# A gated recurrence with top-k experts: contiguous tiles for the transposes, logits in four column groups, exponentials in two batches

## The chip, the cores and the metric

The kernel runs on one core of a Trainium2 chip. The metric is the device time of one execution in microseconds; lower is better. The times given are the median of several runs. One execution was also recorded by the hardware profiler, and the rows below come from that one.

## The reference

Four sequences of 5056 tokens with 256 channels go through a gated recurrence; its output is the input of a mixture of 8 experts, of which each takes only the 80 tokens with the largest gates.

```python
sig = 1.0 / (1.0 + np.exp(-f_logit))
f = lower_bound + (1.0 - lower_bound) * sig
for t in range(S):
    h = f[:, t] * h + (1.0 - f[:, t]) * x[:, t]
    y[:, t] = h
x = y.reshape(B * S, D)                      # 20224 x 256
logits = x @ w_gate                          # 20224 x 8
expert_idx = np.argmax(logits, axis=1)
gate_w = softmax(logits)[arange, expert_idx]
for e in range(8):                           # keep the 80 largest gates of each expert
    h = np.maximum(x[tok_idx] @ w1[e], 0.0)
    out[tok_idx] = gate_w[tok_idx, None] * (h @ w2[e])   # all other rows are zero
```

All of it is in fp32.

## The kernel before

The program has three stages. The first is the recurrence stage. It works on units: 512 tokens of one of the four sequences, with all 256 channels. Four units, one for each sequence, make a group; there are 10 groups and 40 units. The last group of a sequence ends with the sequence and overlaps the one before.

A unit goes through these steps, each a small function that issues its instructions. `load` brings f_logit and x into SBUF through the SP queue; a partition gets four consecutive tokens, 4 KB in one piece. `gate` is a sigmoid on ScalarE (s_t). `enter` multiplies it with x on GpSimd (u_t). `to_channels` transposes both on TensorE, eight 128x128 transposes each, into PSUM tiles sp and up; as a partition holds four consecutive tokens, each transpose writes every fourth column. `decay` makes the factor a from sp on ScalarE, two instructions. `scan` runs the recurrence along 512 tokens on VectorE, two instructions of 128 channels each (shown as one row with x2), into h. `to_tokens` transposes h back with eight transposes into PSUM tiles hp, in two halves of four; ScalarE copies the first half to ht, VectorE the second, and the SP queue stores ht to DRAM. `logits` multiplies h with the gate weights: the weights that the array holds are 128 tokens of h (every fourth column), and 8 columns of wg are streamed. An fp32 product is two passes on TensorE, so the 8 products of a unit are 16 matmuls in the trace.

Once per group, `gates` takes the logits of 4 x 512 tokens: the maximum (mx), the difference from it (sh), an exponential on ScalarE (ex), the first column that reaches the maximum (eq, rv, oh), the sum and its reciprocal (sm, gt), and the gate in the column of its expert (gm). `candidates` transposes gm on TensorE (ct) and copies it to its columns of cand on VectorE.

The order of the instructions on each engine is that in which the program issues them: one loop runs over the units, and each round issues the load of the unit four ahead, the gate and enter of the unit two ahead, to_channels and decay of the next unit, the scan of this unit, to_tokens and logits of the unit before, and the group's steps one and two units later. PSUM has eight banks; before the change sp and up have two buffers each, hp two, and lg and ct one each.

The second stage finds the 80 largest of each row of cand, in ten rounds on VectorE, then again over the lists of one expert; meanwhile the SP queue loads the expert weights and writes zeros to the output. The third stage gathers the chosen tokens, runs the experts on TensorE and scatters the results. Lines 278 to 375 are not changed except for comments.

Of the kernel before, what the change touches and what calls it, by code (L numbers as in the profile page):

```python
# [16 lines left out]
P = 128  # L17
# [5 lines left out]
def kernel(  # L23
# [27 lines left out]
    # The last group of a sequence ends with it and overlaps the one before,  # L51
    # of which only the rows in front of the overlap are used.
# [6 lines left out]
    def rows(g):  # L59
        return used(g) // R  # L60

# [13 lines left out]
    wg = consts.tile([P, DC, E], F32, name="wg")  # L75
    nc.scalar.dma_start(out=wg, in_=w_gate.rearrange("(o p) e -> p o e", p=P))
# [6 lines left out]
    # Candidate row e * C + b * R + r holds the tokens b * S + 4 * pos + r.  # L83
# [8 lines left out]
    cand = consts.tile([P, SEG], F32, name="cand")  # L92
    ctx.enter_context(tc.manual_schedule())

    with tc.tile_pool(name="ld", bufs=5) as ld, \
         tc.tile_pool(name="sup", bufs=3) as sup, \
         tc.tile_pool(name="apool", bufs=2) as apool, \
         tc.tile_pool(name="hpool", bufs=B + 3) as hpool, \
# [6 lines left out]
        xs, fs, sts, uts, sps, ups, decays, hs, lgs, gms = ({} for _ in range(10))  # L105
# [10 lines left out]
        def load(n):  # L116
            g, b = divmod(n, B)
            fs[n] = ld.tile([P, R, D], F32, name="f_t", tag="f_t")
            nc.sync.dma_start(
                out=fs[n], in_=f_logit[b, ds(first(g), G)].rearrange("(p r) d -> p r d", r=R))  # L120
# [12 lines left out]
        def to_channels(n, src, dst, tag):  # L133
            for o in range(DC):
                ps = psu.tile([P, P, R], F32, name=tag, tag=tag)
                for r in range(R):
                    nc.tensor.transpose(ps[:, :, r], src[n][:, r, ds(o * P, P)], ident)  # L137
                dst[n, o] = ps.rearrange("c p r -> c (p r)")
            del src[n]

        # h / (1 - lower_bound) is what runs through the scan.
# [15 lines left out]
        def to_tokens(n):  # L157
            g, b = divmod(n, B)
            n_p = rows(g)
            ht = htok.tile([P, R, D], F32, name="ht", tag="ht")  # L160
            hv = hs[n].rearrange("c o (p r) -> c o p r", r=R)
            half = R // 2
            for i in range(2):
                hp = ptp.tile([P, half, D], F32, name="hp", tag="hp")
                for r in range(half):
                    for o in range(DC):
                        nc.tensor.transpose(hp[:n_p, r, ds(o * P, P)],  # L167
                                            hv[:, o, :n_p, i * half + r], ident)
                copy = nc.scalar.copy if i == 0 else nc.vector.tensor_copy
                copy(ht[:n_p, ds(i * half, half)], hp[:n_p])  # L170
            nc.sync.dma_start(
                out=h_dram[ds(b * S + first(g), n_p * R)].rearrange("(p r) d -> p r d", r=R),
                in_=ht[:n_p])

        def logits(n):
            g, b = divmod(n, B)
            n_p = rows(g)
            if b == 0:
                lgs[g] = plg.tile([P, C, E], F32, name="lg", tag="lg")
            hv = hs[n].rearrange("c o (p r) -> c o p r", r=R)  # L180
# [6 lines left out]
        def gates(g):  # L187
            n_p = rows(g)
            lg = lgs.pop(g)[:n_p]
# [7 lines left out]
            sh = small([C, E], "sh")  # L197
            nc.vector.tensor_tensor(sh, lg, mx.unsqueeze(2).broadcast_to(full), ALU.subtract)  # L198
            ex = small([C, E], "ex")
            nc.scalar.activation(ex, sh, ACT.Exp)  # L200
# [6 lines left out]
            oh = small([C, E], "oh")  # L207
            nc.vector.tensor_tensor(oh, eq, rv.unsqueeze(2).broadcast_to(full), ALU.is_equal)
            sm = small([C], "sm")
            nc.vector.tensor_reduce(sm, ex, AX.X, ALU.add)  # L210
# [3 lines left out]
            gm = small([E, C], "gm")  # L214
            nc.vector.tensor_tensor(gm.rearrange("p e c -> p c e"), oh,
# [191 lines left out]
```

## Time and profile before

| | us |
|---|---|
| median of 3 runs | 553.43 (553.03 to 557.71) |
| span of the profiled execution, first to last instruction | 552.3 |
| TensorE busy in the span | 399.0 |
| VectorE busy | 247.3 |
| ScalarE busy | 150.1 |
| GpSimd busy | 121.6 |
| mean granted TensorE clock, as a share of 2.4 GHz | 0.699 |

The profiled execution's span is 1.1 us shorter than the median of the runs; what lies outside the span isn't shown in the profile. Busy times of engines overlap. In rows of the trace PE is TensorE's matmul, PEld its load of weights, DVE is VectorE, ACT ScalarE, POOL GpSimd. A granted clock of 1.00 is 2.4 GHz, 0.50 is 1.2 GHz. Matmuls are pipelined, and the end of one is modelled, so that a row of several ends a little after the next row has begun.

### The profile page before, as it was taken

How to read it: one execution, taken by the hardware profiler on the slowest of the kernel's cores; microseconds unless marked ns; L12 is line 12 of the kernel's file. 1: busy time of each engine (PE TensorE's matmuls, PEld its weight loads, DVE VectorE, ACT ScalarE, POOL GpSimd, SP SyncE). 2: the span in 40 equal slices, each digit the busy share in tenths (PEclk: the TensorE clock that was granted, in tenths of full speed). 3: DMA queues.
4: the chain of work that ended last, by engine and by line, in shares of the span. 5: the costliest groups of instructions: out<-in, count | busy, mean ns of one | idle time of the engine just before them, and what ended most of it. 6: DMA issues, size and time to landing. Idle time of an engine off the chain costs nothing. (4 is left out here: it accounts for less than half of the span.)

```text
span 552.3 us, 5326 instructions
## 1 busy us (share of the span) xinstructions
PE 399.0 (72%) x2013; PEld 379.1 (69%) x2013; DVE 247.3 (45%) x358; ACT 150.1 (27%) x204; POOL 121.6 (22%) x76
## 2 busy tenths in 40 slices
PE   4998998989989899898998989500000000599996
PEld 4998998989989899898998989400000000578774
DVE  3445334444434344343445443599909993000110
ACT  4544435343353443534445341000000000011100
POOL 5433232213313132222322310200000004500111
PEclk9886767676867767677766886555555555569999
DMA  8766363645636454545546420399999960100000
GB/s 306 266 228 216 127 221 131 219 155 190 213 130 210 166 196 150 193 150 194 193 150 223 144 73 39 142 401 426 435 430 380 379 208 0 48 0 13 13 12 13
DMA packets 31049, 101.93 MB, mean 185 GB/s; under 512 B 3688, under 2 KB 12136, under 8 KB 29744
## 3 DMA queue, kind: packets, MB, share of 16 engines
q1 hardware_dynamic: 29152, 100.15, 49.9%
q0 software_dynamic: 1024, 1.31, 0.9%
q8 instruction: 16, 0.26, 0.2%
q10 hardware_dynamic: 848, 0.13, 0.1%
q14 instruction: 9, 0.07, 0.0%
HBM read 59.43 MB, written 42.16 MB: 184 GB/s over the span
## 5 line engine op out<-in xcount | busy, mean ns | idle before, releaser
L183 PEld LDWEIGHTS lg<-wg,h 128*128 128x128 f32 (+1 forms) x640 | 150.9, 326 | 15.1 <-issue 15.1
L183 PE MATMUL lg<-wg,h 128*128 128x8 f32 (+1 forms) x640 | 149.6, 369 | 12.6 <-DVE sh L198 12.6
L131 POOL TENSOR_TENSOR u_t<-s_t,x_t 128x1024 f32<-128x1024 f32 x40 | 94.1, 2352 | 227.4 <-ACT s_t L127 221.2
L170 DVE COPY ht<-hp 128x512 f32<-128x512 f32 (+1 forms) x40 | 27.7, 691 | 162.3 <-PE hp L167 162.3
L145 ACT ACTIVATE a<-sp,nomlb 128x512 f32<-128x512 f32 x80 | 54.3, 686 | 127.8 <-PE sp L137 97.2
L152 DVE TENSOR_TENSOR_SCAN h<-a,h,up 128x512 f32<-128x512 f32 x72 | 87.8, 1262 | 0.0
L312 PE MATMUL slots<-ident,at2f 8*80 8x8 f32 x1 | 0.2, 231 | 105.0 <-DVE at2f L308 105.0
L137 PE MATMUL sp<-ident,s_t 128*128 128x128 f32 x320 | 72.7, 404 | 3.9 <-ACT s_t L127 3.9
L137 PE MATMUL up<-ident,u_t 128*128 128x128 f32 x320 | 71.9, 393 | 2.5 <-POOL u_t L131 1.7
L312 PEld LDWEIGHTS slots<-ident,at2f 8*80 8x80 f32 x1 | 0.1, 138 | 105.3 <-DVE at2f L308 105.3
L137 PEld LDWEIGHTS sp<-ident,s_t 128*128 128x128 f32 x320 | 65.8, 230 | 4.0 <-ACT s_t L127 4.0
L137 PEld LDWEIGHTS up<-ident,u_t 128*128 128x128 f32 x320 | 61.2, 213 | 8.7 <-PE up L137 3.7
L167 PE MATMUL hp<-ident,h 128*128 128x128 f32 (+1 forms) x320 | 60.0, 349 | 0.0
L357 ACT ACTIVATE hid<-h_ps 128x480 f32<-128x480 f32 (+1 forms) x16 | 6.9, 437 | 181.3 <-remote 130.5
L167 PEld LDWEIGHTS hp<-ident,h 128*128 128x128 f32 (+1 forms) x320 | 55.7, 218 | 0.0
L127 ACT ACTIVATE s_t<-f_t 128x1024 f32<-128x1024 f32 x40 | 42.4, 1059 | 4.9 <-DMA f_t<-in_f_logit_dram 4.8
L170 ACT COPY ht<-hp 128x512 f32<-128x512 f32 (+1 forms) x40 | 23.4, 586 | 69.2 <-PE hp L167 67.7
L354 PE MATMUL h_ps<-xt,w_sb 128*128 128x80 f32 x256 | 36.8, 313 | 6.8 <-issue 4.1
L354 PEld LDWEIGHTS h_ps<-xt,w_sb 128*128 128x128 f32 x256 | 35.7, 227 | 8.0 <-issue 5.5
L282 DVE MAX8 val<-cand 128x8 f32<-128x1264 f32 (+1 forms) x20 | 29.6, 1480 | 14.5 <-DMA cand<-val_dram 13.8
L363 PE MATMUL y_ps<-w_sb,hid 128*80 128x256 f32 x128 | 30.1, 392 | 0.0
L366 DVE TENSOR_SCALAR y<-y_ps,gsl 80x256 f32<-80x256 f32 x8 | 3.8, 480 | 57.9 <-PE y_ps L363 57.9
(53 smaller groups left out, 191.9 us busy)
## 6 DMA issues: line engine op xcount, KB each, us to landing
f_t<-in_f_logit_dram SPq DMA_DIRECT2D x40, 512.0 KB, 4.6
x_t<-in_x_dram SPq DMA_DIRECT2D x40, 512.0 KB, 5.4
h_dram<-ht SPq DMA_DIRECT2D x36, 512.0 KB, 3.0
out_dram<-zero SPq DMA_DIRECT2D x9, 2048.0 KB, 24.4
w_sb<-in_moe_w_dram SPq DMA_DIRECT2D x16, 1024.0 KB, 12.3
h_dram<-ht SPq DMA_DIRECT2D x4, 448.0 KB, 3.3
out_dram<-zero SPq DMA_DIRECT2D x1, 1792.0 KB, 24.4
tok<-id_dram,place POOLq DMA_INDIRECT x8
```

The source lines that it names most:

```text
L127: nc.scalar.activation(sts[n], fs.pop(n), ACT.Sigmoid, scale=-1.0)
L131: nc.gpsimd.tensor_tensor(uts[n], sts[n], xs.pop(n), ALU.mult)
L137: nc.tensor.transpose(ps[:, :, r], src[n][:, r, ds(o * P, P)], ident)
L145: nc.scalar.activation(a, sps.pop((n, o)), ACT.Identity, scale=nomlb[:, ds(o, 1)], bias=1.0)
L152: nc.vector.tensor_tensor_scan(hs[n][:, o], decays.pop((n, o)), ups.pop((n, o)), hs[n - B][:, o, ds(used(n // B - 1) - 1, 1)] if n >= B el ...
L167: nc.tensor.transpose(hp[:n_p, r, ds(o * P, P)], hv[:, o, :n_p, i * half + r], ident)
L170: copy(ht[:n_p, ds(i * half, half)], hp[:n_p])
L183: nc.tensor.matmul(lgs[g][:n_p, b * R + r], hv[:, o, :n_p, r], wg[:, o], start=o == 0, stop=o == DC - 1, skip_group_check=True)
L282: nc.vector.max(out=top, in_=src)
L354: nc.tensor.matmul(h_ps[:, c], w1_sb[e][:, o, ds((c0 + c) * P, P)], xt[:, o], start=o == 0, stop=o == DC - 1, skip_group_check=True)
L357: nc.scalar.activation(hid[:, ds(c0, n)], h_ps[:, :n], ACT.Relu)
L363: nc.tensor.matmul(y_ps, hid[:, c], w2_sb[e][:, c], start=c == 0, stop=c == FC - 1)
```

## The change

The tokens of a unit lie otherwise: a partition gets four tokens that are 128 apart, so that each transpose handles 128 consecutive tokens and writes 128 consecutive columns, and each DMA piece is 1 KB instead of 4 KB. hp has one buffer instead of two.

The logits turn round: the array holds the gate weights (8 columns, padded with zeros to 32), and 128 tokens of h, every fourth column, are streamed. The four values of r go to four groups of 32 columns of the array and so to four groups of 32 partitions of lg. The new step `by_token` brings them back: a copy on ScalarE to ls, and four transposes on TensorE into lt.

`gates` is split. `choice` keeps the maximum, the difference, and the choice of the column, per group, and leaves its results in the tiles shift and chosen. The new `gates` runs twice in the program, after groups 4 and 9: one exponential over five groups, one sum, one reciprocal, and then, for each of the five groups, gm and `candidates`.

```diff
+    def tiles(ap, b, g):
+        return ap[b, ds(first(g), G)].rearrange("(r p) d -> p r d", p=P)
...
-    wg = consts.tile([P, DC, E], F32, name="wg")
+    LC = P // R
+    wg = consts.tile([P, DC, LC], F32, name="wg")
+    nc.vector.memset(wg, 0.0)
...
-         tc.tile_pool(name="ptp", bufs=2, space=PSUM) as ptp, \
+         tc.tile_pool(name="ptp", bufs=1, space=PSUM) as ptp, \
...
-                out=xs[n], in_=x[b, ds(first(g), G)].rearrange("(p r) d -> p r d", r=R))
+                out=xs[n], in_=tiles(x, b, g))
...
-                ps = psu.tile([P, P, R], F32, name=tag, tag=tag)
+                ps = psu.tile([P, G], F32, name=tag, tag=tag)
                 for r in range(R):
-                    nc.tensor.transpose(ps[:, :, r], src[n][:, r, ds(o * P, P)], ident)
+                    nc.tensor.transpose(ps[:, ds(r * P, P)], src[n][:, r, ds(o * P, P)], ident)
...
-                        nc.tensor.transpose(hp[:n_p, r, ds(o * P, P)],
-                                            hv[:, o, :n_p, i * half + r], ident)
+                        nc.tensor.transpose(hp[:, r, ds(o * P, P)],
+                                            hs[n][:, o, ds((i * half + r) * P, P)], ident)
...
         def logits(n):
             g, b = divmod(n, B)
+            if b == 0:
+                lgs[g] = plg.tile([P, B, P], F32, name="lg", tag="lg")
+            hv = hs[n].rearrange("c o (p r) -> c o p r", r=R)
+            for o in range(DC):
+                for r in range(R):
+                    nc.tensor.matmul(lgs[g][ds(r * LC, LC), b], wg[:, o], hv[:, o, :, r],
+                                     start=o == 0, stop=o == DC - 1, skip_group_check=True)
+
+        def by_token(g):
+            ls = gsm.tile([P, B, P], F32, name="ls", tag="ls")
+            nc.scalar.copy(ls, lgs.pop(g))
+            lt = plg.tile([P, B, P], F32, name="lt", tag="lt")
+            for b in range(B):
+                nc.tensor.transpose(lt[:, b], ls[:, b], ident)
+            lts[g] = lt.rearrange("p b (r e) -> p (b r) e", e=LC)[:, :, :E]
...
-            for r in range(R):
-                for o in range(DC):
-                    nc.tensor.matmul(lgs[g][:n_p, b * R + r], hv[:, o, :n_p, r], wg[:, o],
-                                     start=o == 0, stop=o == DC - 1, skip_group_check=True)
...
+        def gates(g0, g1):
+            n = g1 - g0
+            sh = shift[:, ds(g0, n)]
+            nc.scalar.activation(sh, sh, ACT.Exp)
+            sm = gsm.tile([P, n, C], F32, name="sm", tag="sm")
+            nc.vector.tensor_reduce(sm, sh, AX.X, ALU.add)
             nc.vector.tensor_scalar_add(sm, sm, 1e-9)
-            gt = small([C], "gt")
+            gt = gsm.tile([P, n, C], F32, name="gt", tag="gt")
             nc.vector.reciprocal(gt, sm)
...
+            for g in range(g0, g1):
+                n_p = rows(g)
+                gm = gsm.tile([P, E, C], F32, name="gm", tag="gm")[:n_p]
+                nc.vector.tensor_tensor(
+                    gm.rearrange("p e c -> p c e"), chosen[:n_p, g],
+                    gt[:n_p, g - g0].unsqueeze(2).broadcast_to([n_p, C, E]), ALU.mult)
+                gms[g] = gm
+                candidates(g)
...
-            group(gates, n - 2)
-            group(candidates, n - 3)
+            group(by_token, n - 2)
+            group(choice, n - 2)
+            group(lambda g: gates(*batches[g]) if g in batches else None, n - 3)
```

The order of TensorE's instructions for one unit inside a group. Before, the first hp waits for ScalarE, and the second half of hp for nothing outside TensorE (the names behind "waits" are the engines' semaphores):

```order
L137 MATMUL sp<-ident,s_t 128x128 [waits Activation_49]
L137 MATMUL sp<-ident,s_t 128x128 x3
L137 MATMUL up<-ident,u_t 128x128 [waits DVE_49,PE_49,Pool_49]
L137 MATMUL up<-ident,u_t 128x128 x3
L137 MATMUL up<-ident,u_t 128x128 [waits DVE_49,PE_49]
L137 MATMUL up<-ident,u_t 128x128 x3
L167 MATMUL hp<-ident,h 128x128 [waits Activation_49]
L167 MATMUL hp<-ident,h 128x128 x3
L167 MATMUL hp<-ident,h 128x128 [waits PE_49]
L167 MATMUL hp<-ident,h 128x128 x3
L183 MATMUL lg<-wg,h 128x8 x8
```

With the change, from sp of one unit to its logits, at the end of a group, where four transposes lt follow:

```order
L147 MATMUL sp<-ident,s_t 128x128 x8
L147 MATMUL up<-ident,u_t 128x128 [waits DVE_49,Pool_49]
L147 MATMUL up<-ident,u_t 128x128 x3
L147 MATMUL up<-ident,u_t 128x128 [waits DVE_49]
L147 MATMUL up<-ident,u_t 128x128 x3
L175 MATMUL hp<-ident,h 128x128 [waits PE_49]
L175 MATMUL hp<-ident,h 128x128 x3
L175 MATMUL hp<-ident,h 128x128 [waits Activation_49]
L175 MATMUL hp<-ident,h 128x128 x3
L199 MATMUL lg<-h,wg 32x128 [waits Activation_49]
L199 MATMUL lg<-h,wg 32x128 x7
L207 MATMUL lt<-ident,ls 128x128 x4
```

The second half of hp now waits for ScalarE, and the first logits of a new group wait for ScalarE's copy of the old group's.

VectorE at the end of a group, before the change:

```order
L170 COPY ht<-hp 128x512 [waits DMAHW5_49,DVE_49,PE_49]
L196 TENSOR_REDUCE mx<-lg 128x16
L198 TENSOR_TENSOR sh<-lg,mx 128x128 [waits DVE_49]
L202 SCALAR_TENSOR_TENSOR eq<-sh,revexp 128x128 [waits DVE_49]
L206 TENSOR_REDUCE rv<-eq 128x16 [waits DVE_49]
L208 TENSOR_TENSOR oh<-eq,rv 128x128 [waits DVE_49]
L210 TENSOR_REDUCE sm<-ex 128x16 [waits Activation_49]
L211 TENSOR_SCALAR sm<-sm 128x16 [waits DVE_49]
L213 RECIPROCAL gt<-sm 128x16 [waits DVE_49]
L215 TENSOR_TENSOR gm<-oh,gt 128x16x8 [waits DVE_49]
L152 SCALAR_TENSOR_TENSOR h<-a,h,up 128x512 x2
```

The same place with the change:

```order
L178 COPY ht<-hp 128x512 [waits DMAHW1_49,DVE_49,PE_49]
L220 TENSOR_REDUCE mx<-lt 128x16 [waits PE_49]
L222 TENSOR_TENSOR shift<-lt,mx 128x128 [waits DVE_49]
L224 SCALAR_TENSOR_TENSOR eq<-shift,revexp 128x128 [waits DVE_49]
L228 TENSOR_REDUCE rv<-eq 128x16 [waits DVE_49]
L229 TENSOR_TENSOR chosen<-eq,rv 128x128 [waits DVE_49]
L162 SCALAR_TENSOR_TENSOR h<-a,h,up 128x512 [waits Activation_49] x2
```

Four operations have left this place, and the first one now waits for TensorE's transposes lt. They come back in the batch, where VectorE has:

```order
L238 TENSOR_REDUCE sm<-shift 128x80 [waits Activation_49]
L239 TENSOR_SCALAR sm<-sm 128x80 [waits DVE_49]
L241 RECIPROCAL gt<-sm 128x80 [waits DVE_49]
L245 TENSOR_TENSOR gm<-chosen,gt 128x16x8 [waits DVE_49]
L256 COPY cand<-ct 128x128 [waits PE_49]
L245 TENSOR_TENSOR gm<-chosen,gt 128x16x8
L256 COPY cand<-ct 128x128 [waits PE_49]
```

and three more pairs of gm and copy. Each gm stands behind the copy of the group before it, and that copy waits for a transpose on TensorE.

## Rows read from the trace of the kernel before

**Rows 1.** Busy times by stage: PE, PEld, DVE, ACT, POOL; granted clock, DMA share, GB/s.

```profile
40.00:320.00 280.00, 268.13 (x1295) 260.19 (x1293) 118.32 (x177) 117.42 (x154) 75.25 (x32) 0.71 0.52 177
355.30:459.30 104.00, 0.00 (x0) 0.00 (x0) 88.23 (x96) 0.00 (x0) 3.88 (x3) 0.50 0.93 362
459.30:552.30 93.00, 67.70 (x402) 56.98 (x402) 9.43 (x38) 6.89 (x16) 22.13 (x24) 0.81 0.05 15
```

**Rows 2.** The groups by line: busy us, mean ns | idle before it.

```profile
L183 PE MATMUL lg<-wg,h 128*128 128x8 f32 (+1 forms) x640 | 149.6, 369 | 12.6 <-DVE sh L198 12.6
L131 POOL TENSOR_TENSOR u_t<-s_t,x_t 128x1024 f32<-128x1024 f32 x40 | 94.1, 2352 | 227.4 <-ACT s_t L127 221.2
```

**Rows 3.** TensorE's timeline, 107 to 131 us: start, length, what.

```profile
107.68 1.95 PE L137 MATMUL sp<-ident,s_t 128*128 128x128 f32 x8
...
111.10 1.12 PE L167 MATMUL hp<-ident,h 128*128 128x128 f32 x8
112.05 3.78 PE L183 MATMUL lg<-wg,h 128*128 128x8 f32 x16
...
119.13 1.91 PE L167 MATMUL hp<-ident,h 128*128 128x128 f32 x8
122.44 3.87 PE L183 MATMUL lg<-wg,h 128*128 128x8 f32 x16 [1.40 <-DVE sh L198]
```

**Rows 4.** Busy times, columns as in rows 1, in stretches of one granted clock.

```profile
107.70:111.05 3.35, 3.35 (x17) 3.35 (x18) 0.00 (x0) 1.37 (x2) 0.00 (x0) 0.50 0.77 298
111.07:114.47 3.40, 3.40 (x21) 3.40 (x19) 2.22 (x3) 1.54 (x2) 1.08 (x1) 1.00 0.19 76
114.50:117.88 3.38, 3.38 (x17) 3.38 (x18) 0.80 (x1) 0.90 (x2) 1.24 (x1) 0.50 1.00 328
117.90:121.28 3.38, 3.15 (x15) 2.74 (x13) 0.20 (x1) 1.49 (x3) 0.00 (x0) 0.50 0.13 55
```

**Rows 5.** The timeline of all engines, 135.5 to 140.6 us.

```profile
135.56 2.44 DVE L152 TENSOR_TENSOR_SCAN h<-a,h,up 128x512 f32<-128x512 f32 x2
...
136.98 1.90 PE L137 MATMUL up<-ident,u_t 128*128 128x128 f32 x8
...
138.71 1.13 PE L167 MATMUL hp<-ident,h 128*128 128x128 f32 x8
139.39 0.59 ACT L170 COPY ht<-hp 128x512 f32<-128x512 f32 x1 [1.60 <-PE hp L167]
...
139.88 0.69 DVE L170 COPY ht<-hp 128x512 f32<-128x512 f32 x1 [1.87 <-PE hp L167]
140.48 1.27 DVE L152 TENSOR_TENSOR_SCAN h<-a,h,up 128x512 f32<-128x512 f32 x1
```

**Rows 6.** The timeline in the expert stage, clock 1.00.

```profile
508.08 3.62 PE L363 MATMUL y_ps<-w_sb,hid 128*80 128x256 f32 x16
```

**Rows 7.** The timeline: first scan, last scan and the end of the stage.

```profile
10.92 2.33 DVE L152 TENSOR_TENSOR_SCAN h<-a,up 128x512 f32<-128x512 f32 x2 [1.06 <-PE up L137]
...
341.34 2.44 DVE L152 TENSOR_TENSOR_SCAN h<-a,h,up 128x512 f32<-128x512 f32 x2
...
351.68 0.29 DVE L196 TENSOR_REDUCE mx<-lg 128x16 f32<-128x128 f32 x1 [2.82 <-PE lg L183]
...
353.99 0.37 DVE L215 TENSOR_TENSOR gm<-oh,gt 128x128 f32<-128x128 f32 x1
...
354.93 0.29 DVE L224 COPY cand<-ct 128x128 f32<-128x128 f32 x1 [0.57 <-PE ct L222]
...
355.26 1.48 DVE L282 MAX8 val<-cand 128x8 f32<-128x1264 f32 x1
```

**Rows 8.** The groups by line: the exponential and its table.

```profile
L200 ACT ACT_TABLE_LOAD x9 | 11.5, 1283 | 0.2
L200 ACT ACTIVATE ex<-sh 128x128 f32<-128x128 f32 (+1 forms) x10 | 3.1, 311 | 5.5 <-DVE sh L198 5.5
```

**Rows 9.** A stretch while the expert weights of 1 KB pieces (w2) load.

```profile
436.00:438.00 2.00, 0.00 (x0) 0.00 (x0) 1.97 (x3) 0.00 (x0) 0.00 (x0) 0.50 1.09 350
```

More of the change, by code (lines that the diff above doesn't have):

```diff
@@ L74 @@
     nc.scalar.dma_start(out=lb, in_=lower_bound.rearrange("(o p) -> p o", p=P))
-    wg = consts.tile([P, DC, E], F32, name="wg")
-    nc.scalar.dma_start(out=wg, in_=w_gate.rearrange("(o p) e -> p o e", p=P))
+    LC = P // R
+    wg = consts.tile([P, DC, LC], F32, name="wg")
+    nc.vector.memset(wg, 0.0)
+    nc.scalar.dma_start(out=wg[:, :, :E], in_=w_gate.rearrange("(o p) e -> p o e", p=P))
     omlb = consts.tile([P, DC], F32, name="omlb")
@@ L92 @@
     cand = consts.tile([P, SEG], F32, name="cand")
+    BATCHES = 2
+    shift = consts.tile([P, n_grp, C, E], F32, name="shift")
+    chosen = consts.tile([P, n_grp, C, E], F32, name="chosen")
+    nc.gpsimd.memset(shift, 0.0)
     ctx.enter_context(tc.manual_schedule())
@@ L101 @@
          tc.tile_pool(name="psu", bufs=2, space=PSUM) as psu, \
[L102 removed]
+         tc.tile_pool(name="ptp", bufs=1, space=PSUM) as ptp, \
          tc.tile_pool(name="plg", bufs=1, space=PSUM) as plg:
[L105 removed]
+        xs, fs, sts, uts, sps, ups, decays, hs, lgs, lts, gms = ({} for _ in range(11))
         def setup():
@@ L119, in load @@
             nc.sync.dma_start(
-                out=fs[n], in_=f_logit[b, ds(first(g), G)].rearrange("(p r) d -> p r d", r=R))
+                out=fs[n], in_=tiles(f_logit, b, g))
             xs[n] = ld.tile([P, R, D], F32, name="x_t", tag="x_t")
             nc.sync.dma_start(
-                out=xs[n], in_=x[b, ds(first(g), G)].rearrange("(p r) d -> p r d", r=R))
+                out=xs[n], in_=tiles(x, b, g))
         def gate(n):
@@ L166, in to_tokens @@
                     for o in range(DC):
-                        nc.tensor.transpose(hp[:n_p, r, ds(o * P, P)],
-                                            hv[:, o, :n_p, i * half + r], ident)
+                        nc.tensor.transpose(hp[:, r, ds(o * P, P)],
+                                            hs[n][:, o, ds((i * half + r) * P, P)], ident)
                 copy = nc.scalar.copy if i == 0 else nc.vector.tensor_copy
[L170 to L173, printed above, removed]
+                copy(ht[:, ds(i * half, half)], hp)
@@ new lines, in to_tokens @@
+            lap = G - used(g)
+            skip = lap if g == n_grp - 2 else 0
+            out_t = h_dram[ds(b * S + first(g), G)].rearrange("(r p) d -> p r d", p=P)
+            if skip:
+                whole = (G - skip) // P
+                nc.sync.dma_start(out=out_t[:, :whole], in_=ht[:, :whole])
+                part = G - skip - whole * P
+                if part:
+                    nc.sync.dma_start(out=out_t[:part, whole], in_=ht[:part, whole])
+            else:
+                nc.sync.dma_start(out=out_t, in_=ht)
@@ L190, in gates, with choice @@
+        def choice(g):
+            n_p = rows(g)
+            lg = lts.pop(g)[:n_p]
             full = [n_p, C, E]
@@ L196, in gates @@
             nc.vector.tensor_reduce(mx, lg, AX.X, ALU.max)
-            sh = small([C, E], "sh")
+            sh = shift[:n_p, g]
             nc.vector.tensor_tensor(sh, lg, mx.unsqueeze(2).broadcast_to(full), ALU.subtract)
-            ex = small([C, E], "ex")
-            nc.scalar.activation(ex, sh, ACT.Exp)
             eq = small([C, E], "eq")
@@ L232, in group @@
                 f(m // B)
+        ends = sorted({n_grp * i // BATCHES - 1 for i in range(1, BATCHES + 1)} - {-1})
+        batches = {g: (ends[i - 1] + 1 if i else 0, g + 1) for i, g in enumerate(ends)}
         AHEAD = 4
```

22 lines of the change are left out of this document (4 added, 18 removed).

## The prediction

> **What bounds the kernel now.** I read the table by stage first [rows 1]. From 40 to 320 us TensorE computes for 268.13 of 280 us; VectorE for 118, ScalarE for 117, GpSimd for 75, and the DMA engines are half busy. So the recurrence stage is bound by TensorE. The two stages behind it, the search for the largest gates (104 us of VectorE) and the expert products (93 us), are not touched by the change, and nothing in them starts before the last column of the candidates is copied. So I cost only the way to that copy.
>
> Then the groups by line [rows 2]: the logits of line 183 are TensorE's largest group, 149.6 us; GpSimd's multiply takes 2.35 us of each unit. The timeline of TensorE [rows 3] shows one unit (512 tokens of one batch row) in its parts: eight transposes sp in 1.95 us, eight up, eight hp, then 16 logit passes in 3.78 us. Two things are to be seen. A logit pass costs 3.78/16 = 0.236 us; a block of eight transposes costs 1.95 or 1.91 us in one place and 1.12 us in another. The granted clock explains the second [rows 4]: 0.50 (1.2 GHz) where the block takes 1.9, 1.00 (2.4 GHz) where it takes 1.12. The order is telling: the stretch that holds nothing but transposes (107.7 to 111.05) runs at 0.50 and is followed by one at 1.00, and the stretch at 1.00 is spent on logits and is followed by 0.50. Logits with 8 streamed columns do not hold the clock, and they do not use it either: the 16 that begin at 112.05 cross from 1.00 into 0.50 and take no longer (3.78 us) than the 16 at 122.44 (3.87 us). TensorE earns the fast clock with transposes and spends it on logits.
>
> The scans of VectorE mark the units: the first pair starts at 10.92 us, the fortieth at 341.34 us [rows 7], so 39 periods take 330.4 us, 8.47 us each.
>
> **The change, part by part.** *Logits.* The passes stay 16 per unit, but now they load 32 columns of gate weights and stream 128 strided columns of h. No row shows that form. Upper bound: the strided read costs as moving operand what it costs as weights, one pass after another, 3.78 us [rows 3], as before. Lower bound: contiguous streaming costs 3.62/16 = 0.226 us for 256 columns [rows 6], so 0.113 for 128, and four column groups at once leave four such steps, 0.45 us. I take 2.1 us: the read is strided as in line 183, so I stay near 0.236 a pass; but the two passes of one product, which share a column group, stand next to each other in the queue, and the second pass of one product and the first of the next lie in different columns, so I let these overlap: nine steps of 0.236.
>
> *The clock.* The logits now stream 128 columns instead of 8, so I expect a unit to hold the clock at 2.4 GHz, as the stretches of transposes earn it [rows 4]. A block of eight then costs 1.12 with its tail, 0.12 each.
>
> *One buffer for hp instead of two.* The second four hp transposes now wait for ScalarE's copy of the first four. That closes a ring over four engines, and at 2.4 GHz it is longer than TensorE's own work. From the one unit that the trace has at the fast clock [rows 5]: scan to hp 138.71 - 135.56 = 3.15 us (the second half of up waits for the second scan), hp to ScalarE's copy 0.68, the copy 0.59 (new in the ring), a second 0.68 for the other four transposes and the hand-over (before, 139.88 - 139.39 = 0.49 covered it), VectorE's copy to the next scan 0.60. Sum 5.7; with 0.2 for two more hand-overs 5.9 us. TensorE itself: 24 x 0.12 + 2.1 + the wait of about 0.9 for the copy = 5.9. So the two are level, and a unit takes 5.9 us. At 1.2 GHz it would be TensorE: three blocks at 1.7 (1.91 without its tail) + 2.1 + 0.8 = 8.0 us.
>
> *Logits back to tokens and the choice.* Once per group ScalarE copies the logits (0.6 us, beside hp's second half), TensorE makes four more transposes, and VectorE does five small operations. VectorE has them in its queue ahead of the next unit's scans, so the ring stands still: from its copy of hp it waits for logits 2.1 + four transposes and their way out 0.8 - 0.2 = 2.7 us, then five steps of (353.99 - 351.68)/8 = 0.29 us [rows 7], 1.5 us; less the 0.6 that the copy takes anyway: 3.6 us per group, 9 times = 32 us. TensorE idles through much of it, so I charge each group one return of the clock to 1.2 GHz: sp and up at 1.95 instead of 1.12, 1.7 us, of which the ring hides 0.2: 1.5 x 9 = 13.5 us. What leaves is counted in the 330.4: per group two table loads of 1.28 us and an exponential [rows 8], the 1.40 us for which logits waited for sh [rows 3], nine operations of VectorE.
>
> *Exponentials of five groups.* The first batch comes in mid-stage: table load 1.28, 640 elements between 0.31 (128) [rows 8] and five times that, I take 0.75; the sum over 640 elements 0.8; two small ones 0.5; then five rounds gm, transpose, copy into cand, each 354.93 + 0.29 - 353.99 = 1.23 us [rows 7], since every gm stands behind the copy before it: 6.2. All but 0.7 us of ScalarE's part stands on VectorE: 8.3, with the slow clock behind it 9 us. The second batch stands at the end: four rounds more than before (4.9), copy and transposes of logits (1.5), the longer sum (0.5), less the shorter logits (1.6): +5.4 us.
>
> *Tiles of 128 consecutive tokens.* The transposes get contiguous targets, which saves nothing: sp with a step of four in PSUM takes 1.95, hp with contiguous PSUM 1.91 at the same clock [rows 3]. The DMA pieces shrink from 4 KB to 1 KB. The w2 loads have such pieces and run at 350 GB/s [rows 9]; 1.57 MB per unit then need 4.5 us, mixed with stores perhaps 5.2. Both are under 5.9, and loads run four units ahead: no cost, but also little room.
>
> **Sum.** First two periods as before 8; 37 x 5.9 = 218; choice 32; clock 13.5; batch 9: 281 instead of 330, -49. The end +5.4, the first scan +0.5 for 1 KB pieces: -43. Span 552.3 - 43 = 509; the median of the runs, 553.43, is 1.1 above the profiled span, so **511 us**.
>
> **Rivals.** *Serial strided passes* (slower): the four column groups run one after another, and each pass pays for its strided read, 3.78 us per unit. TensorE: 24 x 0.12 + 3.78 + 0.9 = 7.5 us; 37 units 278, choice 34, clock 6 (logits don't care), first two 8, batch 9: 335, +5; the end +7; 565 us. For it: the only strided operand in the trace, line 183, costs 0.236 at either clock where a contiguous one costs 0.113. Against: the outputs lie in four separate groups of columns. It becomes slower than before once logits take more than 3.5 us per unit. Chance 0.2.
>
> *The clock stays divided*: 32 columns of weights keep the array too little busy, and 2.4 GHz is granted half the time, as now (0.71 on average [rows 1]). Then a unit takes the mean of 5.9 and 8.0: +37 x 1.05 = 39, about 548 us. For it: a group's choice and the wait for hp leave gaps. Against: transposes alone raised it in [rows 4]. Chance 0.17.
>
> *Four at once*: logits take under 1 us. The ring still binds at 5.8; the choice is shorter by 1.2 us per group, the end by 1.2, the slow stretches by half: 495 us. The Trainium skill, page TensorE: Matmul & The Clock Gate, section Part 3 (packing small matmuls), has matmuls in different column groups start about 4 ns apart; no row here shows column groups. Chance 0.12.
>
> *Never fast*: transposes don't count for the clock, and a unit stays at 8.0 us: 37 x 2.1 = 78 more, 589 us. That is what the same page says in Part 4 (PE-mode transpose): the fast state does not engage for transposes. The trace disagrees: after a stretch of nothing but transposes at 0.50 comes one at 1.00 [rows 4]. Chance 0.03.
>
> **How the numbers follow.** The forecast has 0.48, the rivals 0.2, 0.17, 0.12 and 0.03. A measurement of this kernel can tell about 1%, 5.5 us. Faster by more: forecast, four at once, and half of the divided clock, 0.69; within 1%: the rest of that and the gentle end of the serial rival, 0.12; slower: 0.19. Range: from 492, four at once with a little less clock loss, to 565, the serial rival's centre.
>
> **What would show it.** Right: scans 5.9 us apart inside a group and about 9.5 across two groups; PEclk near 0.9 from 30 to 290 us; the wait of hp's second half for ScalarE about 0.9 us in all 40 units; candidates complete near 312 us. Wrong: logit passes 0.23 us apart with no overlap (serial rival), PEclk near 0.7 with logits in the slow stretches, or GB/s near 350 in every slice with scans waiting for loads, which would make DMA the bound at about 5 us a unit.

## The result, and the profile after

| | before | after |
|---|---|---|
| median of the runs, us | 555.40 (553.03 to 557.71) | 486.82 (485.79 to 487.55) |
| profiled span, us | 552.3 | 485.1 |
| first scan starts, us | 10.92 | 10.58 |
| 39 periods from the first scan to the last, us | 330.4 | 261.6 |
| last scan to the first MAX8, us | 13.9 | 17.3 |
| first MAX8 to the end, us | 197.0 | 195.6 |

The kernel before was run once more beside the change, so its median is here that of four runs, not of three. The ratio is 0.876, with an interval of 0.871 to 0.881: 12% faster. The forecast was 511 us in a range from 492 to 565, so the kernel is faster than forecast, and 5 us outside the range.

The busy times by stage answer to [rows 1]; columns: stretch, its length, then busy time (instructions) of PE, PEld, DVE, ACT and POOL, granted clock, DMA share, GB/s.

```profile
20.00:270.00 250.00, 180.32 (x1500) 125.82 (x1498) 136.40 (x168) 109.82 (x158) 84.24 (x36) 0.90 0.69 220
272.17:289.46 17.29, 8.14 (x65) 4.11 (x57) 9.88 (x24) 3.78 (x5) 0.17 (x1) 0.80 0.26 92
289.46:393.00 103.54, 0.00 (x0) 0.00 (x0) 87.93 (x96) 0.00 (x0) 3.92 (x3) 0.50 0.91 363
```

TensorE was busy for 96% of its recurrence stage before; now it is for 72%, and the granted clock is 0.90 instead of 0.71. It no longer bounds the stage. The groups by line say the same of the logits: 149.6 us before [rows 2], and now

```profile
L199 PE MATMUL lg<-h,wg 128*32 128x128 f32 x640 | 44.1, 406 | 0.0
```

The timeline of two units follows (start, length, engine, line, what; in brackets the idle time before it and who ended it). The first part is a unit at the lower clock, the second the steady unit; they answer to [rows 3, 5].

```profile
130.34 1.12 PE L199 MATMUL lg<-h,wg 128*32 128x128 f32 x16
130.45 0.69 DVE L178 COPY ht<-hp 128x512 f32<-128x512 f32 x1 [3.85 <-PE hp L175]
131.06 2.44 DVE L162 TENSOR_TENSOR_SCAN h<-a,h,up 128x512 f32<-128x512 f32 x2
131.40 1.85 PE L147 MATMUL sp<-ident,s_t 128*128 128x128 f32 x8
...
135.91 1.10 PE L199 MATMUL lg<-h,wg 128*32 128x128 f32 x16
136.02 0.69 DVE L178 COPY ht<-hp 128x512 f32<-128x512 f32 x1 [2.52 <-PE hp L175]
...
136.62 2.44 DVE L162 TENSOR_TENSOR_SCAN h<-a,h,up 128x512 f32<-128x512 f32 x2
136.94 1.09 PE L147 MATMUL sp<-ident,s_t 128*128 128x128 f32 x8
...
139.12 0.66 PE L147 MATMUL up<-ident,u_t 128*128 128x128 f32 x4 [0.45 <-DVE h L162]
139.61 0.60 PE L175 MATMUL hp<-ident,h 128*128 128x128 f32 x4
140.25 0.59 ACT L178 COPY ht<-hp 128x512 f32<-128x512 f32 x1 [1.35 <-PE hp L175]
...
140.89 0.66 PE L175 MATMUL hp<-ident,h 128*128 128x128 f32 x4 [0.68 <-ACT ht L178]
...
141.58 0.69 DVE L178 COPY ht<-hp 128x512 f32<-128x512 f32 x1 [2.52 <-PE hp L175]
```

Three things are to be seen. The sixteen logit passes take 1.10 us, at either clock (1.12 at the lower one, where the eight sp take 1.85 instead of 1.09). From their start at 135.91 to the first sp at 136.94 TensorE gives them 1.03 us, against 3.78 before. And the ring closes as the prediction drew it: scan 136.62, hp 139.61 (+2.99), ScalarE's copy 140.25 (+0.64), second hp 140.89 (+0.64), VectorE's copy 141.58 (+0.69), and 0.60 to the next scan, as at 136.02 to 136.62. Sum 5.56 us. The logits are not in this chain.

The unit after the last one of a group carries the choice; here VectorE's rows and the multiply of GpSimd beside them (the choice answers to mx and what follows it in [rows 7]).

```profile
120.31 0.69 DVE L178 COPY ht<-hp 128x512 f32<-128x512 f32 x1 [2.52 <-PE hp L175]
121.09 2.35 POOL L141 TENSOR_TENSOR u_t<-s_t,x_t 128x1024 f32<-128x1024 f32 x1 [3.68 <-ACT s_t L137]
...
121.93 0.29 DVE L220 TENSOR_REDUCE mx<-lt 128x16 f32<-128x128 f32 x1 [0.92 <-PE lt L207]
122.25 0.29 DVE L222 TENSOR_TENSOR shift<-lt,mx 128x128 f32<-128x128 f32 x1
...
122.58 1.01 DVE L224 SCALAR_TENSOR_TENSOR eq<-shift,revexp 128x128 f32<-128x128 f32 x1
123.62 0.29 DVE L228 TENSOR_REDUCE rv<-eq 128x16 f32<-128x128 f32 x1
123.94 0.29 DVE L229 TENSOR_TENSOR chosen<-eq,rv 128x128 f32<-128x128 f32 x1
124.15 2.44 DVE L162 TENSOR_TENSOR_SCAN h<-a,h,up 128x512 f32<-128x512 f32 x2
```

The scans stand behind it in VectorE's queue, and TensorE behind the scans. One row is odd: eq takes 1.01 us (0.94 to 1.01 in eight of the ten groups), and 0.29 in the two in which GpSimd is not multiplying. It ends at 123.59, when GpSimd's u_t has ended (123.44).

### The profile page after: what moved, and what is told of

Same layout as the page of the kernel before. It is cut to its first block, busy times and chain, and to the rows that moved or that the text cites. A ratio compares the mean times of both kernels' runs of the same rounds, so it can differ in the third digit from the quotient of the medians.

```text
span 485.1 us, 5330 instructions
## 1 busy us (share of the span) xinstructions
PE 270.0 (56%) x2053; PEld 198.1 (41%) x2053; DVE 251.3 (52%) x335; ACT 131.7 (27%) x192; POOL 123.3 (25%) x77
## 5 line engine op out<-in xcount | busy, mean ns | idle before, releaser
L178 DVE COPY ht<-hp 128x512 f32<-128x512 f32 x40 | 27.7, 692 | 107.4 <-PE hp L175 107.4
L147 PE MATMUL up<-ident,u_t 128*128 128x128 f32 x320 | 56.6, 307 | 40.3 <-DVE h L162 39.0
L175 PE MATMUL hp<-ident,h 128*128 128x128 f32 x320 | 57.0, 306 | 27.1 <-ACT ht L178 27.1
L147 PEld LDWEIGHTS up<-ident,u_t 128*128 128x128 f32 x320 | 38.3, 154 | 57.2 <-issue 32.0
L175 PEld LDWEIGHTS hp<-ident,h 128*128 128x128 f32 x320 | 40.3, 155 | 38.6 <-ACT ht L178 37.8
L147 PE MATMUL sp<-ident,s_t 128*128 128x128 f32 x320 | 47.6, 297 | 4.2 <-ACT s_t L137 4.2
L178 ACT COPY ht<-hp 128x512 f32<-128x512 f32 x40 | 23.5, 586 | 85.5 <-PE hp L175 85.5
L147 PEld LDWEIGHTS sp<-ident,s_t 128*128 128x128 f32 x320 | 38.9, 152 | 15.9 <-issue 11.6
L199 PE MATMUL lg<-h,wg 128*32 128x128 f32 x640 | 44.1, 406 | 0.0
L319 DVE FIND_INDEX8 at<-val,cand 128x8 uint32<-128x1264 f32 (+1 forms) x20 | 29.4, 1470 | 0.0
```

What stands on the lines that cost most here:

```text
L147: nc.tensor.transpose(ps[:, ds(r * P, P)], src[n][:, r, ds(o * P, P)], ident)
L175: nc.tensor.transpose(hp[:, r, ds(o * P, P)], hs[n][:, o, ds((i * half + r) * P, P)], ident)
L178: copy(ht[:, ds(i * half, half)], hp)
L199: nc.tensor.matmul(lgs[g][ds(r * LC, LC), b], wg[:, o], hv[:, o, :, r], start=o == 0, stop=o == DC - 1, skip_group_check=True)
L319: nc.vector.max_index(out=at[:, ds(k, TOP)], in_max=top, in_values=src)
```

## The experiments

The tables below give the ratio to the kernel before, measured on the same chip, with its 95% interval, and the time from one unit's first scan to the next one's, read from the traces: inside a group, for a unit with a choice, for the one after it, and for the one with the batch in mid-stage. An early choice lies one unit later than the others.

| kernel | us | ratio | unit | choice | after it | batch |
|---|---|---|---|---|---|---|
| the change | 486.8 | 0.876 (0.871 to 0.881) | 5.57 | 8.80 | 6.1 to 6.9 | 16.3 |
| old logits, two hp | 559.7 | 1.009 (1.003 to 1.015) | 6.3 to 8.9 | 9.9 to 12.1 | 6.3 to 9.0 | 17.6 |
| old logits, one hp | 602.3 | 1.083 (1.072 to 1.094) | 8.1 to 9.8 | 9.7 to 12.1 | 7.4 to 8.7 | 17.8 |
| old tiles | 492.8 | 0.885 (0.877 to 0.894) | 5.71 | 8.85 | 6.2 to 6.9 | 16.2 |
| exponentials by group | 491.1 | 0.880 (0.873 to 0.888) | 5.57 | 8.80 | 7.8 to 8.9 | none |
| one column group | 570.4 | one run | 7.39 | 13.1 | 6.5 to 6.9 | 16.3 |
| issued by column group | 487.3 | one run | 5.57 | 8.80 | 5.6 to 6.9 | 16.4 |
| contiguous stream | 487.9 | one run | 5.57 | 8.79 | 5.6 to 6.9 | 16.3 |
| two hp | 465.8 | 0.838 (0.830 to 0.846) | 4.73 | 8.85 | 4.7 to 6.0 | 16.4 |
| early choice | 451.3 | 0.812 (0.804 to 0.819) | 5.57 | 5.56 | 5.57 | 15.5 |
| two hp, early choice | 421.8 | 0.756 (0.749 to 0.762) | 4.73 | 5.03 | 4.73 | 15.8 |
| and spread batches | 415.2 | 0.745 (0.739 to 0.752) | 4.73 | 5.03 | 4.73 | 9.6, twice |
| and gm on GpSimd | 405.0 | 0.722 (0.721 to 0.724) | 4.73 | 5.03 | 4.73 | 4.7, twice |

### What each part of the change is worth

*The logits as before*, everything else as after:

```diff
-            for o in range(DC):
-                for r in range(R):
-                    nc.tensor.matmul(lgs[g][ds(r * LC, LC), b], wg[:, o], hv[:, o, :, r],
+            for r in range(R):
+                for o in range(DC):
+                    nc.tensor.matmul(lgs[g][:n_p, b * R + r], hv[:, o, :n_p, r], wg[:, o, :E],
...
-            group(by_token, n - 2)
```

> The changed kernel with the logits as they were before (a block of h as the weights, eight columns streamed, no turn by token), the contiguous tiles and the joined exponentials kept. Theory 1, the gain is the logits': TensorE carries about 2.7 us more a unit again (3.8 against 1.1), a unit takes 7.5 us or more, and the granted clock of the scan stage falls back toward 0.71; 530 to 555 us. Theory 2, the contiguous tiles and the exponentials brought a large part of it: near 490 to 510 us, with the clock near 0.9.

602 us: past the first theory's range, and slower than the kernel before. Of the three things that set it apart from the kernel before (tiles, joined exponentials, a single hp buffer) the buffer looked likeliest. So the next one has the same edit and gives hp its second buffer back (the old logits need no bank for lt):

```diff
-         tc.tile_pool(name="ptp", bufs=1, space=PSUM) as ptp, \
+         tc.tile_pool(name="ptp", bufs=2, space=PSUM) as ptp, \
```

> The kernel with the logits as they were before, contiguous tiles and joined exponentials (602 us), now with two PSUM buffers for hp, as the kernel before had: it is the kernel before with the new tiles and exponentials alone. Theory 1, that kernel was slow because a TensorE that bounds the unit at a divided clock also has to stand for the copy of hp (0.7 us a unit and the clock that it loses by standing): back to 540 to 560 us. Theory 2, the contiguous tiles or the joined exponentials cost by themselves beside the old logits: 580 us or more.

559.7 us, so the first theory holds: beside the old logits one hp buffer costs 43 us. Busy times from 40 to 200 us, first of the kernel with one buffer, then with two (columns as above):

```profile
40.00:200.00 160.00, 143.23 (x673) 136.46 (x672) 59.65 (x69) 49.37 (x68) 37.69 (x17) 0.62 0.52 167
```

```profile
40.00:200.00 160.00, 152.94 (x751) 151.56 (x749) 73.26 (x83) 56.54 (x78) 42.24 (x18) 0.72 0.57 182
```

With one buffer TensorE, the bound, stands for the copy (its matmuls 27.1 us in all 40 units, where with two they do not wait for it), and the granted clock is 0.62 instead of 0.72. The wait alone is 0.68 us a unit; the whole loss is 1.1 us a unit. The lower clock may be the rest; no run shows it by itself.

This also puts a sign on the parts. Tiles and joined exponentials alone give 1.009 of the kernel before: nothing gained, or 1% lost. The new logits, with one buffer on both sides, take 602 to 487.

*The old tiles* (every fourth token, 4 KB pieces), everything else as after:

```diff
-                    nc.tensor.transpose(ps[:, ds(r * P, P)], src[n][:, r, ds(o * P, P)], ident)
-                dst[n, o] = ps
+                    nc.tensor.transpose(ps[:, :, r], src[n][:, r, ds(o * P, P)], ident)
+                dst[n, o] = ps.rearrange("c p r -> c (p r)")
...
-                        nc.tensor.transpose(hp[:, r, ds(o * P, P)],
-                                            hs[n][:, o, ds((i * half + r) * P, P)], ident)
+                        nc.tensor.transpose(hp[:n_p, r, ds(o * P, P)],
+                                            hv[:, o, :n_p, i * half + r], ident)
```

> The changed kernel with tiles of every fourth token (4 KB pieces, strided blocks of h in the transposes back to tokens), new logits and exponentials kept. Theory 1, the layout is worth little: sixteen transposes a unit at 0.12 us in place of 0.11, half of them before the copy that the ring waits for; within 1% of the changed kernel, 484 to 491 us. Theory 2, the contiguous blocks carry part of the gain (strided blocks cost the eight-block passes 1.91 in place of 1.1 us): 38 units times 0.5 us or more, 505 us or above. Theory 3, the 1 KB pieces cost DMA time that the ring feels: 5 us or more faster than the changed kernel.

492.8 us, 1.2% above the change, a little more than the first theory allowed; the intervals of the two ratios overlap, but the units do not: 5.71 against 5.57, and 37 times 0.14 is 5 us. TensorE's timeline of this kernel, inside a group:

```profile
137.66 0.65 PE L177 MATMUL hp<-ident,h 128*128 128x128 f32 x4
138.98 0.75 PE L177 MATMUL hp<-ident,h 128*128 128x128 f32 x4 [0.68 <-ACT ht L180]
```

Four hp take 0.65 and 0.75 where contiguous blocks take 0.60 and 0.66 (139.61 and 140.89 above). Both halves lie in the ring, so 0.05 + 0.09 is the 0.14. Ones at the lower clock [rows 3] could not show this. The transposes sp, whose writes to PSUM have a step of four here, take 1.09 us for eight, as without the step. The 1 KB pieces of the change cost it no time: in its stage no scan, gate or multiply waits for a load after the first few units. They do keep the DMA engines longer: from 40 to 200 us these are busy for 0.70 of the time at 222 GB/s, with 4 KB pieces for 0.61 at 215.

*Exponentials by group*: `BATCHES = 10` in place of 2.

> The changed kernel with the gates' exponentials taken group by group in place of five groups at once. Theory 1, a batch stands on VectorE in front of scans, so ten small ones (table load 1.28 us, exponential 0.3, sum, reciprocal and a round of 1.14 us, some 3.5 to 4 us each) cost nine times 3.5 us in place of the one 10.8, and the end gets some 6 us shorter: 495 to 510 us. Theory 2, a small batch hides in VectorE's wait for hp: the 10.8 and the 6 us are saved, near 470 to 476 us.

491.1 us, between the theories. The unit after a choice now takes 7.8 to 8.9 us; over the stage that is 7.6 us more than the change's one long batch and its shorter returns, and the way from the last scan to the end is 4.0 us shorter (208.9 against 212.9). So joining five groups is worth 4 us. The intervals of the two ratios overlap, so this rests on the two traces; each of the two sums is as the first theory says in kind.

### Where the logits' 1.1 us comes from

*One column group.* All four strides of a unit go to the first thirty-two columns:

```diff
-                    nc.tensor.matmul(lgs[g][ds(r * LC, LC), b], wg[:, o], hv[:, o, :, r],
+                    nc.tensor.matmul(lgs[g][:LC, b], wg[:, o], hv[:, o, :, r],
```

> The changed kernel with all four strides of a unit's logits in the first column group, each overwriting the one before, so that no two passes have columns of their own (the gates are those of one token in four). Theory 1, the four groups run at once and that is what makes the logits 1.1 us: here sixteen passes follow each other at 0.2 us or more, 3.3 us a unit and up; the unit goes from 5.57 to some 7.8 us, 565 to 590 us. Theory 2, passes are short for another reason (thirty-two stationary columns are quick to load): logits near 1.1 to 1.8 us, under 515 us.

570.4 us, the first theory. The same sixteen passes, now in one column group (timeline of this kernel; the first at 1.2 GHz for all but its last 0.9 us, the last at 2.4):

```profile
130.88 3.81 PE L199 MATMUL lg<-h,wg 128*32 128x128 f32 x16
134.63 1.10 PE L147 MATMUL sp<-ident,s_t 128*128 128x128 f32 x8
...
138.30 3.79 PE L199 MATMUL lg<-h,wg 128*32 128x128 f32 x16
```

3.8 us, so 0.23 a pass at either clock (the sixteen that begin at 61.18 us lie wholly at 1.2 GHz and take 3.81 too), which is the old logits' price [rows 3]. The four groups running at once are the whole gain of the logits. The prediction's serial rival said 565 us; that is what it costs when they do not.

*Issued by column group*: the loops over r and o are exchanged, so that the four passes of one group stand in a row.

> The changed kernel with the logits issued by column group (the four passes of one group in a row) in place of by channel block (one pass in each group in turn). Theory 1, passes run at once only where the next in the queue has other columns: the four of a group now follow each other at some 0.2 us, 3.3 us a unit, near 565 us. Theory 2, TensorE looks past a waiting pass: logits still near 1.1 us, within 1% of the changed kernel.

487.3 us: the second theory. A unit's passes take what they took,

```profile
136.45 1.12 PE L199 MATMUL lg<-h,wg 128*32 128x128 f32 x16
```

and the trace has them in rounds of four that start within some 40 ns of each other, a round every 0.2 to 0.24 us, though neighbours in the queue share columns. Which pass of a round is which it does not tell, so how TensorE does it stays open.

*Contiguous stream*: 128 consecutive columns of h are streamed.

```diff
-                    nc.tensor.matmul(lgs[g][ds(r * LC, LC), b], wg[:, o], hv[:, o, :, r],
+                    nc.tensor.matmul(lgs[g][ds(r * LC, LC), b], wg[:, o], hs[n][:, o, ds(r * P, P)],
```

> The changed kernel with the logits streamed from 128 consecutive columns of h in place of every fourth column (the gates then belong to other tokens). Theory 1, the stride sets a round of four at 0.21 us, and without it a round takes some 0.11 us at 2.4 GHz: logits 0.6 us, but the unit hides none of it on TensorE, so 0.4 to 0.5 us a unit if the ring runs through the logits, 466 to 471 us. Theory 2, the ring doesn't run through the logits (scan, hp, copy, next transposes do): 484 to 488 us. Theory 3, a round takes 0.21 us because of the changing of weights: nothing changes.

The time is the second theory's, 487.9 us, with the first theory's passes:

```profile
131.77 0.65 PE L199 MATMUL lg<-h,wg 128*32 128x128 f32 x16
132.34 1.09 PE L147 MATMUL sp<-ident,s_t 128*128 128x128 f32 x8
```

The stride costs 0.46 us of a unit's logits (start to next sp 0.57 instead of 1.03), and the unit is 5.57 us with either. So the ring, not TensorE, sets the unit. The kernel with one column group says how far: its logits take 3.75 - 1.03 = 2.7 us more and its unit 7.39 - 5.57 = 1.8 more, so some 0.9 us more would have been hidden, up to about 1.9 us of logits.

### The ring, the choice and the batch

*Two hp buffers*: ct and bp share lt's bank, which frees one.

```diff
-         tc.tile_pool(name="ptp", bufs=1, space=PSUM) as ptp, \
+         tc.tile_pool(name="ptp", bufs=2, space=PSUM) as ptp, \
...
-            ct = plg.tile([P, P], F32, name="ct", tag="ct")
+            ct = plg.tile([P, B, P], F32, name="ct", tag="lt")[:, 0]
```

> The changed kernel with two PSUM buffers for hp, room made by letting ct and bp use lt's bank. Theory 1, a unit of 5.57 us is a ring: the second half of the transposes to tokens stands until ScalarE has copied the first half (0.68 us a unit); without the wait a unit takes about 4.9 us, 0.65 less, times some 37: near 461 us. Theory 2, another limit lies right behind (ScalarE's gate, copy and decays, or the transfers at 4.4 to 5.2 us a unit): 0.1 to 0.3 us a unit, 475 to 483 us. Theory 3, ct waits for the choice to let go of the bank and holds up TensorE: 487 us or more.

465.8 us, nearest to the first theory. The ring without the wait, in this kernel's timeline:

```profile
103.52 2.44 DVE L162 TENSOR_TENSOR_SCAN h<-a,h,up 128x512 f32<-128x512 f32 x2
...
106.57 1.04 PE L175 MATMUL hp<-ident,h 128*128 128x128 f32 x8
107.21 0.58 ACT L178 COPY ht<-hp 128x512 f32<-128x512 f32 x1 [1.42 <-PE hp L175]
107.65 0.69 DVE L178 COPY ht<-hp 128x512 f32<-128x512 f32 x1 [1.69 <-PE hp L175]
```

The copies of VectorE and ScalarE now overlap, and a unit is 4.73 us, 0.84 less. But a unit with a choice stays at 8.85: there VectorE waits for lt (1.7 us ahead of mx), not for hp, so the gain is 21 us and not 37 times 0.84.

*Early choice*: VectorE's choice behind the next unit's scans.

```diff
             unit(scan, n)
+            group(choice, n - 3)
...
-            group(choice, n - 2)
```

> The changed kernel with the choice of a group moved on VectorE from behind the scans and the copy of one iteration to right behind the scans of the next, where VectorE stood some 2.5 us idle. Theory 1, the 3.2 us that every fourth unit is longer is the choice standing ahead of the next scans, after which TensorE runs on at 1.2 GHz for part of a unit (0.8 to 1.3 us): 9 choices times 3.2 to 4.5 us are 29 to 40 us, 447 to 458 us. Theory 2, the copy of the second half then waits for the choice, and the ring takes the same time through hp: 480 to 490 us.

451.3 us, the first theory. VectorE of this kernel, around a choice:

```profile
130.51 2.44 DVE L162 TENSOR_TENSOR_SCAN h<-a,h,up 128x512 f32<-128x512 f32 x2
132.87 0.26 DVE L220 TENSOR_REDUCE mx<-lt 128x16 f32<-128x128 f32 x1
133.16 0.29 DVE L222 TENSOR_TENSOR shift<-lt,mx 128x128 f32<-128x128 f32 x1
133.49 0.29 DVE L224 SCALAR_TENSOR_TENSOR eq<-shift,revexp 128x128 f32<-128x128 f32 x1
...
134.14 0.29 DVE L229 TENSOR_TENSOR chosen<-eq,rv 128x128 f32<-128x128 f32 x1
135.46 0.69 DVE L178 COPY ht<-hp 128x512 f32<-128x512 f32 x1 [1.03 <-PE hp L175]
```

lt is there when VectorE comes to it, eq finds GpSimd idle and takes 0.29, and VectorE still waits 1.03 us for hp behind it. All units but those of the batch are equal: the slow units after a choice are gone too, and the granted clock from 40 to 200 us is 0.97 instead of 0.87.

*Both*: the two edits above together.

> The changed kernel with both remedies: two PSUM buffers for hp, and the choice behind the next scans. Theory 1, they add up: a unit of 4.73 us as in the kernel with two buffers, no longer fourth unit, 38 units times 0.84 us under the kernel with the early choice: 418 to 425 us. Theory 2, at 4.7 us VectorE has no idle place left that takes a whole choice (2.3 to 3 us): units with a choice are 1 us or more longer, 428 to 440 us. Theory 3, the transfers bind (4.4 to 5.2 us a unit at their rate): 5.2 us a unit, near 440 us.

421.8 us: they add up, as the first theory says; the second is there in small, 0.3 us on the unit that holds the choice. The batch is the one long unit left.

*Both, and spread batches*: four, four and two groups; exponentials at the end of one unit, sums and products behind the next scans, transposes at that unit's end, copies in the one after. Its core:

```diff
             unit(scan, n)
             group(choice, n - 3)
+            batch(gates, n - 4)
+            batch(candidates, n - 5)
...
-            group(lambda g: gates(*batches[g]) if g in batches else None, n - 3)
+            batch(exps, n - 3)
+            turn()
```

> The kernel with both remedies, and the exponentials in three batches (four, four and two groups), each spread over three units: exponentials behind a unit's copy, sums, reciprocals and products behind the next scans, the turns to candidates at the end of that unit, their copies one unit later. Theory 1, the 10 us of the batch in the middle shrink to 1 to 2 us for each batch and the end after the last scan from 17.3 to some 11 us: 12 to 15 us less than with both remedies alone, 404 to 411 us. Theory 2, ScalarE's table loads (2 times 1.28 us a batch) then bind and the batches cost as much as before: 418 us or more.

415.2 us, half of what the first theory promised: each of the two batches in mid-stage takes a unit of 9.62 us, 4.9 more than the others. The timeline there:

```profile
102.86 0.55 DVE L243 RECIPROCAL gt<-sm 128x64 f32<-128x64 f32 x1
103.34 1.25 ACT L155 ACTIVATE a<-sp,nomlb 128x512 f32<-128x512 f32 x2
103.45 5.31 DVE L247 TENSOR_TENSOR gm<-chosen,gt 128x128 f32<-128x128 f32 x4
103.51 5.02 POOL L141 TENSOR_TENSOR u_t<-s_t,x_t 128x1024 f32<-128x1024 f32 x2 [5.51 <-ACT s_t L137]
...
108.61 0.67 DVE L178 COPY ht<-hp 128x512 f32<-128x512 f32 x1
```

The products gm of four groups, 0.37 us each when alone, take 5.31 us, and nothing that they read is late: sums and reciprocals are done. The first and the third take 0.39 and 0.37; the second and the fourth take 2.53 and 2.48, and each ends 0.2 us after one of GpSimd's two multiplies. The table loads (1.28 us each, at 99.14 and 101.08) make those two come late and back to back. Hence the last kernel:

*gm on GpSimd*, and the transposes one unit later, so that TensorE does not wait for it:

```diff
-                nc.vector.tensor_tensor(
+                mul = nc.gpsimd if g1 < n_grp else nc.vector
+                mul.tensor_tensor(
...
-            batch(candidates, n - 5)
+            batch(candidates, n - 6)
...
-            turn()
+            batch(turn, n - 5)
```

> The kernel with both remedies and spread batches (415 us), with the products gm of the first two batches on GpSimd in place of VectorE, turned one unit later. Theory 1, a product of two SBUF operands on VectorE stands still while GpSimd multiplies (four products that take 0.3 us each alone took 5.31 us beside two u_t), so the unit of a batch falls from 9.6 us to 5 to 6 us: 7 to 9 us less in all, 406 to 409 us. Theory 2, the batch unit is long because ScalarE's two table loads make the gate of a later unit late: the unit stays 8 us or more, 412 us or above.

405.0 us, a little better than the first theory; the unit of a batch is as long as a plain one (4.73). The table loads are still there. Both edits were made at once; what the later transposes do alone was not run. The same place:

```profile
103.74 2.38 POOL L141 TENSOR_TENSOR u_t<-s_t,x_t 128x1024 f32<-128x1024 f32 x1 [5.54 <-ACT s_t L137]
103.94 0.69 DVE L178 COPY ht<-hp 128x512 f32<-128x512 f32 x1 [0.29 <-PE hp L175]
104.54 2.44 DVE L162 TENSOR_TENSOR_SCAN h<-a,h,up 128x512 f32<-128x512 f32 x2
...
106.08 1.51 POOL L248 TENSOR_TENSOR gm<-chosen,gt 128x128 f32<-128x128 f32 x4
```

GpSimd makes the four products in 1.51 us between two of its multiplies, and the scan beside them takes its usual 2.44. The recurrence stage of this kernel, 40 to 200 us:

```profile
40.00:200.00 160.00, 141.37 (x1390) 105.41 (x1392) 119.75 (x159) 101.21 (x145) 76.51 (x40) 1.00 0.94 305
```

The clock is 1.00 throughout, and the DMA engines are busy for 0.94 of the time: what is left there is small for whoever speeds up an engine alone. What 4 KB pieces would give here was not run.

## Why the prediction was off

The mechanism held: the time came from the recurrence stage alone, through shorter logits and a held clock, to a ring, over VectorE, TensorE and ScalarE (three engines, not the four of the prediction). The sizes did not. Terms in us, as the prediction's sum has them:

| term | predicted | measured |
|---|---|---|
| first scan | 11.4 | 10.6 |
| first two periods | 8 | 8.8 |
| 37 units | 37 x 5.9 = 218 | 37 x 5.57 = 206 |
| choice, 9 times | 32 | 8 x 3.23 + 2.5 = 28.4 |
| units slowed after it | 13.5 | 7.9 |
| batch | 9 | 10.8 |
| last scan to MAX8 | 19.3 | 17.3 |
| the rest | 197.0 | 195.6 |

- **The unit: the step that failed.** It was taken as 5.9 us twice over, as a ring of 5.7 and 0.2 for hand-overs, and as TensorE's own work with logits of 2.1. The ring measures 5.56: its step from scan to hp was read from a unit that still had up at 1.9 us [rows 5] (3.15 there, 2.99 now, and 2.99 too with the old tiles at 2.4 GHz), and the hand-overs were already in the start-to-start times. That is 12 of the 24 us. TensorE's side of the sum was not needed: up to about 1.9 us of logits are hidden.
- **The logits' 2.1 us** was a middle between bounds of 3.78 and 0.45, by a story of which passes could overlap. Measured are 1.03, and 0.57 without the stride. It costs little in the unit, as just said, but 1.1 us in each choice, where VectorE waits for the logits: 1.62 us from its copy to mx (120.31 to 121.93) instead of 2.7. The choice was off by 0.4 us only, since eq took 0.7 us more than reckoned.
- **The clock** came as forecast, 0.90, and the return to 1.2 GHz after a choice is there (1.85 us for sp), but costs 0.5 to 1.3 us and not 1.5. The early choice shows its cause: with no stop for the choice the slow units vanish.
- **The batch** was taken as 9 us and measures 10.8. The second of its five gm alone adds 1.7: it takes 2.05 us instead of 0.36, beside GpSimd's multiply.

```profile
160.58 2.34 POOL L141 TENSOR_TENSOR u_t<-s_t,x_t 128x1024 f32<-128x1024 f32 x1 [10.30 <-ACT s_t L137]
161.10 2.05 DVE L245 TENSOR_TENSOR gm<-chosen,gt 128x128 f32<-128x128 f32 x1
```

- **The rivals.** *Four at once* was the true case, at a chance of 0.12; its 495 us kept a ring of 5.8 and so was high by the same error. The Trainium skill, page TensorE: Matmul & The Clock Gate, Part 3, has such passes start about 4 ns apart; here neighbours of one round start 7 ns apart (median of the traced starts), and at 2.4 GHz a round follows every 0.23 us with a strided stream and 0.11 with a contiguous one (medians too). *Serial strided passes* did not occur. Its sum came near (565, measured 570 with one column group), in part by luck: nine choices add 52 us there, not 34, and the unit after a choice is 0.5 to 0.9 us shorter than a plain one, where the sum has 6 us in all for slow units. *The clock stays divided* is out at 0.90, *never fast* as well.
- **Tiles** were taken to save nothing, by a comparison of writes at 1.2 GHz; they save 0.14 us a unit at 2.4 GHz, where hp reads h. The 1 KB pieces cost the units nothing, as forecast, and the 0.5 us for them at the first scan did not come.

The parts, in the experiments' order, are: tiles and joined exponentials by themselves nothing or 1% against it, the second hp buffer given up +43 us, the new logits -115. Once the logits are short, tiles are worth 6 us and joined exponentials 4, and the buffer 21.

## What to carry to other kernels

Price a bank or buffer that an edit gives up on its own: here it cost 43 us beside a bound TensorE, 21 beside a free one, and the shared bank next to nothing (16.4 us for the batch instead of 16.3). When the bound engine gets faster, write out the ring that remains start to start, in rows at the clock that the new kernel will have, and add nothing for hand-overs that those times already hold. Small operations that stand ahead of the next scans in an in-order queue cost their whole wait; put them where their engine is known to wait for somebody else.

## What the runs showed that was not expected

**VectorE stands still beside GpSimd when both its operands lie in SBUF.** eq, from two SBUF tiles, takes 0.29 us where GpSimd is idle and 1.01 while it multiplies; gm 0.37 against 5.31 for four; scans and copies, whose second operand or whose source is in PSUM, keep their 1.22 and 0.69 us. Off VectorE, gm costs the unit nothing. The Trainium skill, page SBUF — State Buffer, section Who interferes with whom, has this rule: a VectorE instruction with two SBUF inputs and a GpSimd instruction that reads SBUF share a port, and whichever comes second waits for the other's end. The traces agree: eq and gm end 0.15 and 0.2 us after GpSimd's multiply, and the gm that starts just before one (103.45 against 103.51) takes its 0.39.

**A strided fp32 stream does not follow the clock.** Sixteen strided passes take 1.10 us at 2.4 GHz and 1.12 at 1.2 in four column groups, 3.79 and 3.81 in one, while transposes beside them go from 1.09 to 1.85. Contiguous, they take 0.65 at 2.4 GHz and 1.08 at 1.2 in four groups, so at the lower clock the stride costs next to nothing.
